# Two attention and MLP layers on one core: reordered first and last stages in place of a pre-scaled third term of VectorE's exponential

## The chip, the cores and the metric

The kernel runs on one core of one Trainium2 chip. The metric is the device time of one execution in microseconds. Before the change the median of three runs is 1617.62 us (1613.32 to 1618.33); the profiled execution, on which all positions in this text are based, took 1613.32 us and has a span of 1611.5 us from the first to the last instruction. TensorE had a mean granted clock of 0.997.

## The reference

Two rounds of the same two blocks, with the same weights, on x of 2048 rows and 512 columns in bf16. There are 32 heads of 16 columns, and the MLP has 1792 hidden columns.

```python
def _A_ref(x, wqkv, wo):                     # attention
    qkv = (x @ wqkv).reshape(B, S, 3, H, Dh).transpose(2, 0, 3, 1, 4)
    q, k, v = qkv[0], qkv[1], qkv[2]
    scores = jnp.einsum("bhqd,bhkd->bhqk", q, k) * (Dh ** -0.5)
    p = _softmax(scores, axis=-1)
    o = jnp.einsum("bhqk,bhkd->bhqd", p, v)
    return o.transpose(0, 2, 1, 3).reshape(B, S, D) @ wo

def _B_ref(x, w1, w2):                       # MLP
    h = jnp.maximum(x @ w1, 0)
    return h @ w2

x = A_x
x = x + _A_ref(_layernorm(x), A_wqkv, A_wo)
x = x + _B_ref(_layernorm(x), B_w1, B_w2)
x = x + _A_ref(_layernorm(x), A_wqkv, A_wo)
x = x + _B_ref(_layernorm(x), B_w1, B_w2)
```

The heads are narrow and the rows many: per layer there are 32 x 2048 x 2048 exponentials, and they are the largest single piece of work.

## The kernel before

Scores are computed with the keys on the partitions: 128 keys by 512 queries of one head are one block, which fills one bank of PSUM (128 x 512 fp32). A *slot* is up to three blocks in one of two PSUM tiles `ps_s` of three banks. ScalarE (ACT in the profile) takes the exp of a slot into one of five buffers `e`, and TensorE multiplies that with the values into `ps_o` (32 partitions per head, four heads side by side); a column of ones beside the values gives the sum for the division. The kernel's Python code holds its own model of the engines' clocks and uses it to decide, slot by slot, in what order to emit score products, value products and all the projection and MLP work that fills TensorE in between.

Some slots hand their third block to VectorE (DVE), which works out the exponential itself. Two such blocks of 512 columns make a *pair* of 128x1024. The score, scaled to powers of two, is turned into a 16-bit integer whose bits, read as bf16, are a straight-line 2^x (`lin`); the same bits with the mantissa masked off are the power of two below it (`step`); and a cubic of the mantissa is the third part (`cube`). The exponential is the sum of the three, and since the value product is linear, TensorE adds them up: three value products for a block of VectorE's against one for a block of ScalarE's. The factor `CUBE` of the third part can be put on the part itself or on the values:

```python
    CUBE, SUM = 0.1667, 2.16619
    THIRD = (8, 9, 10, 11)
    vthird = {kb: sb([P, H // 2, PW], BF16, f"vthird_{kb}") for kb in THIRD}
    # scale_v: vthird[kb] = vaug[l][kb] * CUBE, one operation of 128x544 per kb and layer
    ...
    def pv(sg, kb, g, rhs, p=None):
        values = vthird[kb] if p and p["scaled"] else vaug[sg["l"]][kb]
        nc.tensor.matmul(ps_o[32 * g : 32 * g + 32, 0 : sg["w"]],
            values[:, 4 * sg["T"] + g, 2 * e : 2 * e + 32], rhs, ...)
    ...
    def chain(p):      # after both halves of lin are there
        steps = (
            (342, lambda: bits(0x7F, 0x3F80)),                           # mantissa into step
            (609, lambda: nc.vector.tensor_mul(out=power, in0=mantissa, in1=mantissa)),
            (342, lambda: nc.vector.tensor_scalar(
                out=power, in0=power, scalar1=CUBE, scalar2=None, op0=ALU.mult)),
            (342, lambda: bits(0x7F80, 0)),                              # step
            (609, lambda: nc.vector.tensor_mul(
                out=power.bitcast(BF16), in0=power, in1=line.bitcast(BF16))),
        )
        nos = (0, 1, 3, 4) if p["scaled"] else range(5)
```

For a pair whose two blocks both lie in key blocks 8 to 11, the third product uses the scaled values and the chain leaves out the scaling. The choice of the block for VectorE prefers such key blocks, and looks ahead in the list of units for one. A pair begins only if the model finds VectorE's queue (`BACKLOG`, `queued`) short enough for it to be done in time.

The layer norm takes its inverse root on VectorE from an integer first guess and, at the two ends of the kernel, three Newton steps there:

```python
    def ln_stats(tag, tt, i):
        nc.vector.bn_stats(out=st[:], in_=x_t[tt][:])
        nc.vector.bn_aggr(out=mv[ln_n(tag)][:, i, :], in_=st[:])
    def ln_rstd(tag, part):     # part 0: 3 operations; parts 1 to 3: a Newton step of 3 each
```

The first stage, up to the first exp:

```python
    idle_matmuls(18)            # keep TensorE's clock up; another one behind each transpose
    for i in range(TPC): ln_stats(tag, i, i)
    for part in range(4): ln_rstd(tag, part)
    for i in range(TPC): ln_apply(tag, i, i)
    for i in range(TPC):        # transpose, copied by VectorE (even i) and ScalarE (odd i)
        ...
    b = plain(k_mms(0, 0));     nc.scalar.copy(out=ktp[0][0][0][:], in_=b)
    b = plain(q_mms(0, 0, 0));  q_masked(0, b, 0); q_masked(0, b, 1)       # VectorE
    for kb in range(2):
        b = plain(v_mms(kb));   nc.scalar.copy(out=v_out(0, kb), in_=v_in(b))
```

The last stage, after the loop over the slots, works on the last 256 rows (two tiles of 128, `rows`):

```python
    while seg_at[0] < len(segs):
        force_v(); run_dve(0.0, musts)        # last value products, copy of ps_o to u
    ending[0] = True
    run_all()                                 # all groups still waiting
    for i in rows:                            # residual + products with wo of 7 of 8 parts
        add(banks[i], ident[:], x_t[tt + i][:], True, False)
        for t in range(NT - 1):
            add(banks[i], ot[t][:, part(i)], wo[:, t // 2, :], False, False)
    for i in rows:
        last_steps[0](i)                      # shuffle of u (once), reciprocal, product -> ot[7]
        add(banks[i], ot[NT - 1][:, part(i)], wo[:, (NT - 1) // 2, :], False, True)
        nc.scalar.copy(out=x_t[tt + i][:], in_=at_bank(banks[i]))
    for i in rows: ln_stats(tag, tt + i, i)
    for step in range(4): ln_rstd(tag, step)
    for i in rows: ln_apply(tag, tt + i, i)
    half_part(0, range(NF))                   # output of an earlier tile of rows
    ...                                       # transposes; then the last MLP, 14 steps:
    for ft in range(NF + 1):
        ... w1buf[n % NW1][:, c, :] ...       # 4 buffers; load_w1(n + NW1) refills behind each
    ...                                       # two copies, two stores from SyncE's queue
```

The softmax here doesn't subtract the row's maximum and nothing guards it: scores larger than these inputs give would overflow.

## Time and profile before

| | ScalarE | VectorE | TensorE | GpSimd |
|---|---|---|---|---|
| busy, us of 1611.5 | 1566.0 | 1496.8 | 1451.6 | 93.8 |
| instructions | 1387 | 3007 | 14667 | 279 |

| stage, us from the start of the span | what happens | length |
|---|---|---|
| 0 to 16.81 | loads, first layer norm, first keys, queries and values | 16.81 |
| 16.81 to 1577.83 | 1366 exps on ScalarE, everything else beside them | 1561.02 |
| 1577.83 to 1611.50 | last normalisation, last layer norm, last MLP, stores | 33.67 |

The stages are cut at the start of the first exp and at the end of the last. The profile names an operation by its line, its engine, what it writes and reads (`e<-ps_s`: from a PSUM tile of scores into a buffer of exponentials), its shape and its count; then follow the busy time, the mean duration of one in ns, and the idle time of the engine just before, with what ended it. Neighbouring operations on one engine overlap, so a mean duration can be longer than the step from one start to the next, and 703 x 1573 ns is more than the 1052.1 us in which any of those exps was running. A timeline row has the start and the length in us, the engine and line, the operation, and a count if neighbours are merged; in brackets stands the idle time before it and what released it. In the rows of the stages, each engine has its busy time and, in brackets, its number of instructions; the last three numbers are TensorE's granted clock, the share of the DMA engines and the GB/s moved.

### The profile page before, as it was taken

How to read it: one execution, taken by the hardware profiler on the slowest of the kernel's cores; microseconds unless marked ns; L12 is line 12 of the kernel's file. 1: busy time of each engine (PE TensorE's matmuls, PEld its weight loads, DVE VectorE, ACT ScalarE, POOL GpSimd, SP SyncE). 2: the span in 40 equal slices, each digit the busy share in tenths (PEclk: the TensorE clock that was granted, in tenths of full speed). 3: DMA queues.
4: the chain of work that ended last, by engine and by line, in shares of the span. 5: the costliest groups of instructions: out<-in, count | busy, mean ns of one | idle time of the engine just before them, and what ended most of it. 6: DMA issues, size and time to landing. Idle time of an engine off the chain costs nothing.

```text
span 1611.5 us, 35252 instructions
## 1 busy us (share of the span) xinstructions
PE 1451.6 (90%) x14667; PEld 508.9 (32%) x14863; DVE 1496.8 (93%) x3007; ACT 1566.0 (97%) x1387; POOL 93.8 (6%) x279
## 2 busy tenths in 40 slices
PE   8888888999989999899998998888989999899997
PEld 3222222322222222222222222222333333344444
DVE  7669999999999999999898998999999999999994
ACT  6999999999999999999999999999999999999993
POOL 2000001001010011000100000001001010010100
PEclk9999999999999999999999999999999999999999
DMA  5000000210002100021000100000210111121223
GB/s 164 1 1 2 2 2 10 46 28 12 5 18 45 21 15 9 12 47 25 9 1 17 31 1 1 2 3 9 44 30 16 26 29 36 22 48 36 47 46 73
DMA packets 113889, 39.97 MB, mean 25 GB/s; under 512 B 103328, under 2 KB 111264, under 8 KB 113728
## 3 DMA queue, kind: packets, MB, share of 16 engines
q1 hardware_dynamic: 101696, 26.21, 7.1%
q0 software_dynamic: 10688, 10.18, 3.4%
q8 instruction: 116, 1.90, 0.5%
q10 hardware_dynamic: 1344, 1.31, 0.2%
q14 instruction: 45, 0.37, 0.1%
HBM read 24.38 MB, written 2.10 MB: 16 GB/s over the span
## 4 chain that ended last, share of the span: by engine, by line
ACT 78%; PE 11%; DVE 7%; issue 3%; DMA 1%; ACTq 0%; DVEq 0%
ACT e L1311 78%; PE ps_s L1302 4%; PE ps_o L901 3%; PE ps_f L434 3%; DVE lin L995 2%; DVE step L1036 1%; PE ps_s L1365 1%; DVE cube L1047 1%; DVE cube L1051 1%; DVE stats L465 0%; DVE ht L682 0%; DVE q L625 0%; DVE ot L836 0%; DVE x L708 0%; DMA c<-u 0%
## 5 line engine op out<-in xcount | busy, mean ns | idle before, releaser
L1311 ACT ACTIVATE e<-ps_s 128x1024 bf16<-128x1024 f32 (+1 forms) x1366 | 1554.8, 1367 | 6.6 <-PE ps_s L1302 4.7
L1302 PE MATMUL ps_s<-q,ktp 32*128 32x512 bf16 (+1 forms) x6060 | 601.2, 341 | 106.7 <-ACT e L1311 84.7
L901 PE MATMUL ps_o<-e,vaug 128*32 128x512 bf16 (+1 forms) x4284 | 494.7, 345 | 11.3 <-DVE u L823 4.8
L995 DVE TENSOR_SCALAR lin<-ps_s 128x512 int16<-128x512 f32 x662 | 452.6, 686 | 35.8 <-PE ps_s L1302 30.4
L1302 PEld LDWEIGHTS <-ktp 32*128 32x128 bf16 x6060 | 189.9, 91 | 504.5 <-issue 375.6
L1036 DVE TENSOR_SCALAR step<-lin 128x1024 int16<-128x1024 int16 x662 | 262.9, 420 | 3.3 <-PE ps_o L901 0.6
L901 PEld LDWEIGHTS <-vaug 128*32 128x32 bf16 x6004 | 161.5, 94 | 302.2 <-issue 291.5
L1047 DVE TENSOR_TENSOR cube<-step 128x1024 f16<-128x1024 bf16 x331 | 225.9, 685 | 2.7
L1051 DVE TENSOR_TENSOR cube<-cube,lin 128x1024 bf16<-128x1024 f16 x331 | 225.5, 682 | 0.0
L901 PE MATMUL ps_o<-step,vaug 128*32 128x512 bf16 (+1 forms) x836 | 143.2, 340 | 0.3 <-issue 0.3
L901 PE MATMUL ps_o<-cube,vthird 128*32 128x512 bf16 (+1 forms) x788 | 138.2, 337 | 0.6 <-issue 0.3
L901 PE MATMUL ps_o<-lin,vaug 128*32 128x512 bf16 (+1 forms) x836 | 127.4, 338 | 4.1 <-DVE u L823 2.8
L434 PE MATMUL ps_f<-xnT,w 128*128 128x512 bf16 (+1 forms) x446 | 116.9, 345 | 5.6 <-issue 2.5
L434 PE MATMUL ps_f<-w,ht 128*128 128x512 bf16 x334 | 104.8, 384 | 5.6 <-issue 4.3
L850 POOL DMA_DIRECT2D r<-u x52 | 37.5, 721 | 1165.9 <-DVE step L1036 424.3
L434 PE MATMUL ps_f<-xnT,wqkv 128*128 128x512 bf16 (+1 forms) x288 | 82.3, 359 | 6.4 <-issue 2.5
L682 DVE TENSOR_SCALAR ht<-ps_f 128x512 bf16<-128x512 f32 x103 | 70.7, 687 | 3.2 <-PE ps_f L434 3.0
L434 PE MATMUL ps_f<-wo,ot 128*128 128x512 bf16 x206 | 65.4, 384 | 3.0 <-issue 1.9
L625 DVE TENSOR_SCALAR q<-ps_f,qmask 128x512 bf16<-128x512 f32 (+1 forms) x102 | 64.8, 661 | 3.1 <-PE ps_f L434 3.0
L434 PEld LDWEIGHTS <-w 128*128 128x128 bf16 x504 | 39.1, 97 | 60.0 <-issue 50.6
L836 DVE SCALAR_TENSOR_TENSOR ot<-u,mask,r 128x512 bf16<-128x512 f32 (+2 forms) x82 | 51.3, 627 | 1.1
L901 PEld LDWEIGHTS <-vthird 128*32 128x32 bf16 x788 | 39.8, 95 | 32.8 <-issue 30.1
(91 smaller groups left out, 609.8 us busy)
## 6 DMA issues: line engine op xcount, KB each, us to landing
w<-in_B_w_dram SPq DMA_DIRECT2D x140, 128.0 KB
r<-u POOLq DMA_DIRECT2D x25, 256.0 KB, 7.1
r<-u POOLq DMA_DIRECT2D x27, 128.0 KB, 4.5
out_dram<-x SPq DMA_DIRECT2D x16, 128.0 KB
x<-in_A_x_dram SPq DMA_DIRECT2D x14, 128.0 KB
w<-in_B_w_dram SPq DMA_DIRECT2D x1, 1792.0 KB
wqkv<-in_A_wqkv_dram ACTq DMA_DIRECT2D x2, 512.0 KB
c<-u SPq DMA_DIRECT2D x48, 8.0 KB
```

Of the source, the lines that this page charges most:

```text
L434: nc.tensor.matmul(out, lhsT, rhs, start=i % k == 0, stop=i % k == k - 1)
L625: return nc.vector.tensor_scalar(out=qbuf[n % 2][e][:, 0:w], in0=b, scalar1=qmask[e][:, 0:1], scalar2=None, op0=ALU.mult,)
L682: nc.vector.tensor_scalar(out=out, in0=sums, scalar1=0.0, scalar2=None, op0=ALU.max)
L836: nc.vector.scalar_tensor_tensor(out=ot[t][:, at_column + a : at_column + a + w], in0=u[:, a : a + w], scalar=mask[e][:, 0:1], in1=r[:, a ...
L850: nc.gpsimd.dma_start(out=r[:, 0:width], in_=bass.AP(tensor=sums.tensor, offset=sums.offset, ap=[list(sums.ap[0]), [0, 32], [1, width]],),)
L901: nc.tensor.matmul(ps_o[32 * g : 32 * g + 32, 0 : sg["w"]], values[:, 4 * sg["T"] + g, 2 * e : 2 * e + 32], rhs, start=g not in sg["begun" ...
L995: first = nc.vector.tensor_scalar(out=lin[which][:, half * QS : (half + 1) * QS], in0=src, scalar1=EXP_BIAS, scalar2=0.0, op0=ALU.add, op1 ...
L1036: nc.vector.tensor_scalar(out=stair, in0=line, scalar1=keep, scalar2=put, op0=ALU.bitwise_and, op1=ALU.bitwise_or,)
L1047: (609, lambda: nc.vector.tensor_mul(out=power, in0=mantissa, in1=mantissa)),
L1051: (609, lambda: nc.vector.tensor_mul(out=power.bitcast(BF16), in0=power, in1=line.bitcast(BF16))),
L1302: nc.tensor.matmul(b[:, a : a + sg["w"]], kt[32 * g : 32 * g + 32, kc : kc + P], qbuf[sg["n"] % 2][sg["e"]][32 * g : 32 * g + 32, 0 : sg[" ...
L1311: ex = nc.scalar.activation(out=eb[:, 0 : place[m]], in_=b[:, 0 : place[m]], func=ACTF.Exp, scale=1.0 / (LOG2E * UNIT),)
```

## The change

Two things of different kinds are exchanged.

*Taken out* is the pre-scaled third part: `THIRD`, the scaled value copies, their eight scaling operations, the search for blocks in those key blocks, and the chain of four operations; every pair has all five again.

*Put in* is a set of measures at the two ends, to shorten the chains there. At the start the statistics of four tiles run one behind the other and are aggregated together; the inverse root takes a cubic first step and one Newton step (nine operations with the first guess, in place of twelve); the idle products between the transposes go; the first value block is copied by VectorE between the two query masks, and the second comes later. At the end the residual products of one row of tiles stand ahead of the last value product, the last normalisation reads PSUM instead of a copy, and groups that still wait are emitted behind the layer norm. The MLP's first weights are kept for the last stage: four in their buffers and ten in buffers of the first layer's keys, which are free by then. MLP inputs have a buffer of their own, `xn2T`. The last store but one and the last are issued from two engines.

Cut to its core (`...` marks cuts):

```diff
+GAIN = 64.0 / 9.0
-    THIRD = (8, 9, 10, 11)
-    vthird = {kb: sb([P, H // 2, PW], BF16, f"vthird_{kb}") for kb in THIRD}
+    xn2T = sb([P, NDC, QS], BF16, "xn2T")
...
-        nc.vector.bn_stats(out=st[:], in_=x_t[tt][:])
-        nc.vector.bn_aggr(out=mv[ln_n(tag)][:, i, :], in_=st[:])
+        nc.vector.bn_stats(out=stats[ln_n(tag)][:, i, :], in_=x_t[tt][:])
+    def ln_seed(tag, rows, gain=1.0):        # aggregates of all rows, then 2 operations
+    def ln_root(tag, rows):                  # seed, then 7 operations on VectorE
+        nc.vector.tensor_mul(out=t1, in0=y, in1=y)
+        nc.vector.tensor_mul(out=t1, in0=t1, in1=a)
+        stt(out=t1, in0=t1, scalar=-10.0 / 3.0, in1=t1, op0=ALU.add, op1=ALU.mult)
+        stt(out=y, in0=t1, scalar=5.0, in1=y, op0=ALU.add, op1=ALU.mult)
+        stt(out=t1, in0=y, scalar=-0.5 / GAIN, in1=y, op0=ALU.mult, op1=ALU.mult)
+        nc.vector.tensor_mul(out=t1, in0=t1, in1=a)
+        stt(out=y, in0=t1, scalar=1.5, in1=y, op0=ALU.add, op1=ALU.mult)
...
-        if n < len(chunks) * NF:
+        if n < len(chunks) * NF - NF + NW1:                       # load_w1
...
+        if (l, j) == (1, LAST - 2):                               # weights of the last stage
+            for ft in range(NF): ... w1_last.append(home); if ft >= NW1: nc.sync.dma_start(out=home, ...)
...
-        nos = (0, 1, 3, 4) if p["scaled"] else range(5)
+        for n, (cost, fn) in enumerate(steps):
...
-    idle_matmuls(18)
+    idle_matmuls(21)
-        copy = nc.scalar.copy if i % 2 else nc.vector.tensor_copy
+        copy = nc.vector.tensor_copy if i > 1 else nc.scalar.copy
-        idle_matmuls(1)
...
+    uses(q_masked(0, q_bank, 0), at_q)
+    b = plain(v_mms(0))
+    uses(nc.vector.tensor_copy(out=v_out(0, 0), in_=v_in(b)), in_bank[0])
+    uses(q_masked(0, q_bank, 1), at_q)
-    for kb in range(2):
-        b = plain(v_mms(kb))
-        uses(nc.scalar.copy(out=v_out(0, kb), in_=v_in(b)), in_bank[0])
...
-        order = sorted(sg["kbs"], key=lambda kb: len(sg["kbs"]) == NKB and kb in THIRD)
-        for kbs in zip(*[iter(order)] * both):
+        for kbs in zip(*[iter(sg["kbs"])] * both):
...
-        for sg, kb, g in now:
-            run_until(("v", sg["l"], kb))                         # values ready before each slot
...
+    first_part(0)                                                 # residual products, row 0
+    while seg_at[0] < len(segs):
+        force_v()                                                 # last value product
+        run_dve(0.0, musts)
+    first_part(1)
     for i in rows:
         last_steps[0](i)                                          # now reads ps_o, not u
...
+    ln_root(tag, n_rows)
     for i in rows:
         ln_apply(tag, tt + i, i)
+    ending[0], wide[0] = True, False
+    run_all()                                                     # stood ahead of all this before
...
-        nc.sync.dma_start(
+        (nc.scalar if i % 2 else nc.sync).dma_start(
```

## The prediction

> **What bounds the kernel now.** I read the page's busy line first, then the chain that ended last, then the span cut into three stages at the first and last exp, then the groups by shape, and last the timeline of the two ends.
>
> ```profile
> PE 1451.6 (90%) x14667; PEld 508.9 (32%) x14863; DVE 1496.8 (93%) x3007; ACT 1566.0 (97%) x1387; POOL 93.8 (6%) x279
> ...
> ACT 78%; PE 11%; DVE 7%; issue 3%; DMA 1%; ACTq 0%; DVEq 0%
> ```
>
> ScalarE (ACT) is busy for 97% of the span and makes 78% of the chain; VectorE (DVE) comes next with 93%. The stage view (length, then busy time and count of each engine) separates three parts:
>
> ```profile
> 0.00:16.81 16.81, 12.57 (x60) 5.50 (x61) 13.16 (x42) 4.42 (x7) 2.41 (x35) 1.00 0.78 252
> 16.81:1577.83 1561.02, 1412.80 (x14450) 488.82 (x14642) 1471.17 (x2931) 1554.85 (x1366) 91.40 (x244) 1.00 0.10 21
> 1577.83:1611.50 33.67, 26.25 (x166) 14.61 (x160) 12.43 (x35) 6.72 (x14) 0.00 (x0) 0.97 0.29 71
> ```
>
> Between the first exp at 16.81 us and the end of the last at 1577.83 us ScalarE runs 1366 exps and nothing else, with 1561.02 - 1554.85 = 6.2 us idle. That stage is as long as its exps are wide. The other two stages, 16.8 and 33.7 us, are chains of dependent work in which ScalarE hardly counts. So I add up three separate changes: the width of the exps, the start, the end. The groups by shape carry the first:
>
> ```profile
> L1311 ACT ACTIVATE e<-ps_s 128x1536 bf16<-128x1536 f32 x703 | 1052.1, 1573 | 4.5 <-PE ps_s L1302 2.8 <-PE ps_o L901 1.2
> L1311 ACT ACTIVATE e<-ps_s 128x1024 bf16<-128x1024 f32 x662 | 717.7, 1148 | 2.1 <-PE ps_s L1302 1.9 <-PE ps_o L901 0.2
> L995 DVE TENSOR_SCALAR lin<-ps_s 128x512 int16<-128x512 f32 x662 | 452.6, 686 | 35.8 <-PE ps_s L1302 30.4
> L1036 DVE TENSOR_SCALAR step<-lin 128x1024 int16<-128x1024 int16 x662 | 262.9, 420 | 3.3 <-PE ps_o L901 0.6
> L1047 DVE TENSOR_TENSOR cube<-step 128x1024 f16<-128x1024 bf16 x331 | 225.9, 685 | 2.7
> L1051 DVE TENSOR_TENSOR cube<-cube,lin 128x1024 bf16<-128x1024 f16 x331 | 225.5, 682 | 0.0
> L1048 DVE TENSOR_SCALAR cube<-cube 128x1024 f16<-128x1024 f16 x24 | 10.1, 420 | 0.2
> ```
>
> Each slot has three score blocks of 512 columns. In 703 slots ScalarE takes all three; in 662 it takes two and VectorE one. VectorE joins two such blocks to a pair, so there are 331 pairs, and only 24 of them need the scaling step of line 1048.
>
> **What the Trainium skill says.** "Perfetto Trace Analysis", section Identifying the Most-Contended Engine, says to improve the engine with the highest occupancy; the trace agrees that it is ScalarE, with VectorE so near that it matters who does which block. The same page, Optimizing Scalar/DVE Operations, says that both engines pay a fixed cost per instruction, so larger operations are cheaper per element. The trace agrees: 512 more columns add 1573 - 1148 = 425 ns to an exp, though two thirds of the wider exp's duration would be 1049 and not 1148. "VectorE: DVE Perf Modes", The perf-mode tier table, gives a one-source operation in SBUF a faster mode than one with two tensors; the trace has 420 ns for the scaling against 682 to 685 for the products. "DMA: Bandwidth & Descriptors", Issuing engines are not separate DMA queues, says that a second issuing engine saves the issue alone; no run here has shown it.
>
> **Part 1: the third part of VectorE's pairs goes.** Without the scaled copy of the values every pair needs the scaling again. The scheduler that writes the program, seeing a longer queue, gives VectorE fewer pairs. The instruction list of the changed program has 749 exps of 1536 columns, 616 of 1024 and one of 512, 308 pairs and 308 scalings.
>
> ScalarE: 46 exps become 512 columns wider. By the mean durations that is 46 x 0.425 = 19.6 us. The step between exps gives a check: the first 18, all wide, take 24.28 us, so (24.28 - 1.57) / 17 = 1.336 us a step; the 662 narrow ones then have (1560.2 - 703 x 1.336) / 662 = 0.938, and 46 x 0.398 = 18.3 us. I take **+19 us**, all on the bound.
>
> VectorE, by the same mean durations: gone are 46 x 0.686 + 46 x 0.420 + 23 x 1.367 = 82 us and 2.3 us of scaled copies; new are 284 x 0.420 = 119 us. That is +35 us of durations; they overlap, with operations of 128x512 starting 0.60 us apart where one lasts 0.69, so about +25 to +30 us of occupied time. In an exp stage of 1580 us VectorE goes from 1471 / 1561 = 94% to about 95%. TensorE has 92 fewer value products of a block, four of which run side by side: about 5 us less. Neither ends the stage, so I count nothing for them.
>
> **Part 2: the start.** The lines of the head that set the first exp:
>
> ```profile
> 6.72 0.18 DVE L466 BATCH_NORM_AGGREGATE mv<-stats 128x2 f32<-128x6 f32 x1
> ...
> 9.32 1.38 DVE L507 TENSOR_SCALAR xn<-x,mv,ya 128x512 bf16<-128x512 bf16 x4
> ...
> 14.10 1.41 DVE L625 TENSOR_SCALAR q<-ps_s,qmask 128x512 bf16<-128x512 f32 x2 [0.17 <-PE ps_s L1103]
> ...
> 16.37 0.39 PE L1302 MATMUL ps_s<-q,ktp 32*128 32x512 bf16 x3
> ```
>
> Four statistics in a row, then four aggregates, save three waits of about 0.1 us, and nine small operations replace twelve at 0.2 us: apply starts near 8.5, not 9.32. The transposes follow it without idle matmuls between, and ScalarE's two copies come first: I put the key product at 10.8 us, where it was 12.18. Key and query take 1.9 us (12.7). VectorE then does the first mask (to 13.4), the copy of the first values (to 14.4) and the second mask (to 15.0). The score product waits for that second mask, since its bank is in the tile that the scores overwrite. Before, the mask ended at 15.5, but TensorE worked off eleven value products first and scores began at 16.37. So scores at 15.1, exp 0.44 later: 15.5, **-1.3 us**.
>
> **Part 3: the end.** E is the end of the last exp.
>
> ```profile
> 1583.98 0.38 PE L1365 MATMUL ps_s<-x,ident 128*128 128x512 bf16 x1 [0.85 <-DVE x L708]
> ...
> 1587.85 1.07 ACT L1375 CAST x<-ps_s 128x512 bf16<-128x512 f32 x2 [7.10 <-PE ps_s L1365]
> ...
> 1592.59 0.74 DVE L507 TENSOR_SCALAR xn<-x,mv,ya 128x512 bf16<-128x512 bf16 x2
> ...
> 1594.39 1.03 PE L1365 MATMUL ps_s<-xnT,w 128*128 128x256 bf16 x8 [0.39 <-DVE xnT L1406]
> ```
>
> Before: two MLP groups and one output group hold TensorE until the residual products can start at E+6.2; the copies come at E+10.0, apply at E+14.8, the last MLP at E+16.6. After: the first row's eight products (1.7 us) run beside the last exp, the last value product follows near E+1.2 and ends at E+1.7. The shuffle reads PSUM directly. Shuffle, two reciprocals and two products took 1583.85 to 1586.91, 3.06 us: done at E+4.8. Last product and copy of the second row: E+5.8. Its statistics 0.7, aggregate and nine small operations 2.1: apply at E+8.7. TensorE meanwhile has the rest of one output group and all of the other, 9 + 15 products of 0.22 us, until about E+10.4, later than apply; so transposes start there, and after 1.2 us of copies the last MLP starts at E+11.6: -4.9 us. Its weights are all in place, so the wait for them at 1601.70 goes (0.31 us on TensorE, about 0.5 in step): -0.5. The two last stores issue from two engines, where one took 0.83 us for both: -0.2. Together **-5.6 us**.
>
> **Sum.** +19 - 1.3 - 5.6 = +12 us on the median 1617.62: about 1629.5; I say 1629.
>
> **The rivals.** *The stage was losing time to waits, which go.* Pairs go wherever the scheduler can fit blocks, and the old rule, every value product's input ready before the slot, is dropped. For it: in the trace the shortest steps between exps are 1.330 and 0.904 us, so 1561 us holds about 27 us over 703 x 1.330 + 662 x 0.904. Against it: ScalarE's idle time is 6.2 us, and nothing in the change aims at the rest. If half of the 27 went, 1616. *VectorE becomes the bound.* For it: a fifth step in nearly every pair, 95% busy, and 84.7 us in which scores wait for exps show how tightly the buffers turn. Late lines hold score banks, and ScalarE then idles. Against it: the program has 23 fewer pairs just for that. It would cost 10 to 20 us more: 1640 to 1650. *The start is held by a transfer.* The first values are now ahead of the second mask, and their weights are the last part of that load to arrive, at 12.7 us in the trace before, just when I need them. It would cost up to 1 us.
>
> **Range and chances.** The exp term is a count times a measured step, good to about 1 us if the waits stay; the waits may move by 8 either way; the ends are good to 2; the runs before span 1613.3 to 1618.3. That gives 1620 to 1640. Faster by 2% means under 1585, which no rival reaches; slower by 2% means over 1650, which only a late VectorE reaches.
>
> **What would show it.** Exp stage about 1580 us with 749 wide exps and under 10 us idle; first exp near 15.5; last exp to the end near 28 us, the last MLP starting some 11.6 us after the last exp with no wait for weights. I am wrong if the step of a wide or narrow exp moves by over 10 ns, or if scores wait for VectorE's lines.

## The result and the profile after

The changed kernel takes 1629.52 us (median of 4 runs, 1628.83 to 1631.42); the kernel before, run beside it, 1615.47 (4 runs). The ratio is 1.0089, with a 95% interval of 1.0065 to 1.0113: slower by about 14 us, and within 2%. The prediction was 1629.0.

The busy line and the chain by engine, from the page of the changed kernel:

```profile
PE 1457.4 (90%) x14553; PEld 509.3 (31%) x14743; DVE 1507.5 (93%) x3126; ACT 1583.3 (97%) x1383; POOL 93.9 (6%) x279
...
ACT 77%; DVE 10%; PE 9%; issue 2%; DMA 1%; POOL 0%; SPq 0%; ACTq 0%; DVEq 0%
```

ScalarE still bounds the kernel, and it is busy 17.3 us longer (1566.0 before). The three stages, cut again at the first exp and at the end of the last (length, then busy time and count of each engine, TensorE's clock, DMA share, GB/s):

```profile
0.00:16.83 16.83, 12.26 (x52) 5.06 (x54) 11.07 (x34) 3.15 (x5) 2.42 (x35) 0.90 0.84 266
16.83:1599.45 1582.62, 1421.92 (x14361) 491.70 (x14548) 1485.11 (x3062) 1574.67 (x1366) 91.50 (x244) 1.00 0.10 22
1599.45:1627.90 28.45, 23.26 (x141) 12.55 (x142) 11.36 (x31) 5.52 (x13) 0.00 (x0) 1.00 0.06 19
```

The exp stage is 21.6 us longer, the last stage 5.2 us shorter, and the first, in this execution, the same. The groups by shape:

```profile
L1298 ACT ACTIVATE e<-ps_s 128x1536 bf16<-128x1536 f32 x749 | 1116.9, 1594 | 10.5 <-PE ps_s L1289 8.3 <-PE ps_o L914 2.0
L1298 ACT ACTIVATE e<-ps_s 128x1024 bf16<-128x1024 f32 x616 | 678.2, 1169 | 1.5 <-PE ps_s L1289 1.3
L1021 DVE TENSOR_SCALAR lin<-ps_s 128x512 int16<-128x512 f32 x616 | 421.4, 687 | 25.5 <-PE ps_s L1289 20.0 <-issue 0.2
...
L1069 DVE TENSOR_TENSOR cube<-step 128x1024 f16<-128x1024 bf16 x308 | 210.7, 686 | 1.5 <-PE ps_o L914 0.3
L1073 DVE TENSOR_TENSOR cube<-cube,lin 128x1024 bf16<-128x1024 f16 x308 | 210.1, 683 | 0.0
L1070 DVE TENSOR_SCALAR cube<-cube 128x1024 f16<-128x1024 f16 x308 | 129.2, 421 | 1.0
```

749 wide exps instead of 703, 308 pairs instead of 331, and the scaling in every pair at 421 ns. The shortest steps from one exp to the next are those of before, 1.330 us for 1536 columns and 0.904 for 1024. With them 46 wider exps are 46 x 0.426 = 19.6 us. What the stage takes above the sum of its shortest steps I call its **waits**: 26.8 us before, 28.8 now. 19.6 + 2.0 is the 21.6.

The head, from the timeline of the changed kernel:

```profile
8.07 1.38 DVE L504 TENSOR_SCALAR xn<-x,mv,ya 128x512 bf16<-128x512 bf16 x4
...
10.52 3.31 PE L1121 MATMUL ps_s<-xnT,wqkv 128*128 128x512 bf16 x8 [0.62 <-DMA x<-in_A_x_dram]
...
15.60 0.74 DVE L612 TENSOR_SCALAR q<-ps_s,qmask 128x512 bf16<-128x512 f32 x1
...
16.39 0.40 PE L1289 MATMUL ps_s<-q,ktp 32*128 32x512 bf16 x3 [1.44 <-DVE q L612]
```

Apply starts 1.25 us earlier (9.32 before) and the key product at 10.52, both 0.3 to 0.4 us earlier than predicted. Then eight products take 3.31 us, where 1.89 was expected. Three cuts through the head show why; the last three columns are TensorE's granted clock, DMA share and GB/s:

```profile
10.00:12.00 2.00, 1.48 (x5) 0.61 (x6) 1.56 (x4) 0.04 (x1) 0.00 (x0) 0.70 0.76 225
12.00:14.00 2.00, 2.00 (x6) 0.68 (x5) 0.13 (x1) 0.59 (x1) 0.00 (x0) 0.50 0.73 219
14.00:16.00 2.00, 0.95 (x4) 0.34 (x3) 1.63 (x3) 0.00 (x0) 0.00 (x0) 0.94 0.92 285
```

The clock was down to half; in the kernel before it was 1.00 in all three cuts. So the gain of the start was lost in this execution. Other programs with the same head, below, kept it; of the changed kernel itself no other execution was profiled.

The tail, E being the end of the last exp at 1599.45:

```profile
1601.59 0.44 DVE L879 STREAM_SHUFFLE r<-ps_o 128x256 f32<-128x256 f32 x1
...
1605.13 0.59 ACT L1366 CAST x<-ps_s 128x512 bf16<-128x512 f32 x1 [0.66 <-PE ps_s L1349]
...
1607.09 3.19 PE L1349 MATMUL ps_s<-w,ht 128*128 128x512 bf16 x14
...
1608.48 0.73 DVE L504 TENSOR_SCALAR xn<-x,mv,ya 128x512 bf16<-128x512 bf16 x2
...
1610.12 0.61 PE L513 MATMUL ps_s<-ident,xn 128*128 128x128 bf16 x8
...
1611.44 1.03 PE L1349 MATMUL ps_s<-xn2T,w 128*128 128x256 bf16 x8 [0.28 <-ACT xn2T L1399]
```

The shuffle starts at E+2.1 (E+6.0 before), the second copy at E+5.7, apply at E+9.0, and the last MLP at E+12.0 instead of E+16.6. Apply ended 0.9 us before the transposes began: TensorE was busy with an output group (the 14 products), as predicted.

### The profile page after: what moved, and what is told of

It is laid out like the page before. It is cut to its first block, busy times and chain, and to the rows that moved or that the text cites. A ratio compares the mean times of both kernels' runs of the same rounds, so it can differ in the third digit from the quotient of the medians.

```text
span 1627.9 us, 35135 instructions
## 1 busy us (share of the span) xinstructions
PE 1457.4 (90%) x14553; PEld 509.3 (31%) x14743; DVE 1507.5 (93%) x3126; ACT 1583.3 (97%) x1383; POOL 93.9 (6%) x279
## 4 chain that ended last, share of the span: by engine, by line
ACT 77%; DVE 10%; PE 9%; issue 2%; DMA 1%; POOL 0%; SPq 0%; ACTq 0%; DVEq 0%
ACT e L1298 77%; DVE lin L1021 3%; PE ps_s L1289 3%; PE ps_o L914 2%; PE ps_f L430 2%; DVE step L1061 1%; DVE cube L1069 1%; PE ps_s L1349 1%; DVE cube L1073 1%; DVE cube L1070 1%; DVE q L612 0%; DVE ht L669 0%; DMA u<-c 0%; DMA wqkv<-in_A_wqkv_dram 0%; DVE ot L843 0%
## 5 line engine op out<-in xcount | busy, mean ns | idle before, releaser
L1298 ACT ACTIVATE e<-ps_s 128x1536 bf16<-128x1536 f32 (+1 forms) x1366 | 1574.7, 1402 | 12.0 <-PE ps_s L1289 9.6
L914 PE MATMUL ps_o<-e,vaug 128*32 128x512 bf16 (+1 forms) x4340 | 516.9, 346 | 13.6 <-DVE u L827 4.6
L1021 DVE TENSOR_SCALAR lin<-ps_s 128x512 int16<-128x512 f32 x616 | 421.4, 687 | 25.5 <-PE ps_s L1289 20.0
L1061 DVE TENSOR_SCALAR step<-lin 128x1024 int16<-128x1024 int16 x616 | 246.1, 421 | 0.9 <-PE ps_o L914 0.7
L1069 DVE TENSOR_TENSOR cube<-step 128x1024 f16<-128x1024 bf16 x308 | 210.7, 686 | 1.5 <-PE ps_o L914 0.3
L1073 DVE TENSOR_TENSOR cube<-cube,lin 128x1024 bf16<-128x1024 f16 x308 | 210.1, 683 | 0.0
L914 PE MATMUL ps_o<-cube,vaug 128*32 128x512 bf16 (+1 forms) x780 | 145.5, 341 | 0.5 <-issue 0.5
L1070 DVE TENSOR_SCALAR cube<-cube 128x1024 f16<-128x1024 f16 x308 | 129.2, 421 | 1.0
L430 PE MATMUL ps_f<-xn2T,w 128*128 128x512 bf16 (+1 forms) x457 | 121.1, 343 | 9.5 <-DVE ht L669 3.6
L612 DVE TENSOR_SCALAR q<-ps_f,qmask 128x512 bf16<-128x512 f32 (+1 forms) x102 | 65.1, 662 | 10.1 <-PE ps_f L430 7.9
L843 DVE SCALAR_TENSOR_TENSOR ot<-u,mask,r 128x512 bf16<-128x512 f32 (+1 forms) x78 | 49.8, 640 | 0.9
```

The source lines that it names most:

```text
L430: nc.tensor.matmul(out, lhsT, rhs, start=i % k == 0, stop=i % k == k - 1)
L612: return nc.vector.tensor_scalar(out=qbuf[n % 2][e][:, 0:w], in0=b, scalar1=qmask[e][:, 0:1], scalar2=None, op0=ALU.mult,)
L843: nc.vector.scalar_tensor_tensor(out=ot[t][:, at_column + a : at_column + a + w], in0=u[:, a : a + w], scalar=mask[e][:, 0:1], in1=r[:, a ...
L914: nc.tensor.matmul(ps_o[32 * g : 32 * g + 32, 0 : sg["w"]], vaug[sg["l"]][kb][:, 4 * sg["T"] + g, 2 * e : 2 * e + 32], rhs, start=g not in ...
L1021: first = nc.vector.tensor_scalar(out=lin[which][:, half * QS : (half + 1) * QS], in0=src, scalar1=EXP_BIAS, scalar2=0.0, op0=ALU.add, op1 ...
L1061: nc.vector.tensor_scalar(out=stair, in0=line, scalar1=keep, scalar2=put, op0=ALU.bitwise_and, op1=ALU.bitwise_or,)
```

## The experiments

Each compares with the kernel before, run on the same chip. Some have short names below: third_out and third_in are the kernels with the third part taken out and put back, new_start and new_end those with one end of the change alone, and combined is the changed kernel with the third part and the early pairs. Where I write of waits, first exp or last stage, they are from the profile of that kernel, counted as above.

### The third part alone taken out

```diff
 (the kernel before)
-    THIRD = (8, 9, 10, 11)
+    THIRD = ()
```

> The kernel before with the pre-scaled third part taken out and nothing else changed: no key block counts as scaled, so every pair does its own scaling. The program has 739 exps of 1536 columns and 626 of 1024 (703 and 662 before), 313 pairs. If the width of the exps is all that counts: 36 x 0.41 = +15 us in the exp stage, so about 1576 us of it, first and last stage as before (16.8 and 33.7 us), some 15 us or 0.9% slower than before. If VectorE became the bound, ScalarE's idle time in the stage rises above 15 us and the time is 25 us or more above before. If the stage had waits to win back, it is under 8 us slower. The changed kernel has 10 blocks fewer on VectorE than this one, so part of its exp time would then come from something else than the third part.

Measured: 1629.32 us, ratio 1.0091 (1.0075 to 1.0107), which is the whole loss. But the program has 739 wide exps, not 749:

```profile
L1311 ACT ACTIVATE e<-ps_s 128x1536 bf16<-128x1536 f32 x739 | 1106.5, 1586 | 5.0 <-PE ps_s L1302 3.0 <-PE ps_o L901 1.7
```

Its exp stage:

```profile
16.70:1596.15 1579.45, 1451.08 (x14561) 492.62 (x14561) 1503.21 (x3106) 1569.75 (x1366) 91.25 (x244) 1.00 0.10 21
```

So the third part accounts for 36 of the 46. 36 x 0.426 = 15.3 us, waits 29.9 (+3.1), last stage 30.4 instead of 33.7 (-3.2): together the 15.1 us by which the profiled span grew. What the change puts in is then worth nothing on the whole, though its last stage is 2 us shorter than this one's. Something in it must cost what its ends gain.

### The third part put back into the changed kernel

```diff
 (the changed kernel; the last norm's own buffer xn2T makes room for it)
+    THIRD = (8, 9, 10, 11)       # and scaled copies, four-step chains, search for blocks, as before
-    xn2T = sb([P, NDC, QS], BF16, "xn2T")
```

> The changed kernel with the pre-scaled third part put back; so that it fits in SBUF, the MLP inputs go back into the attention's buffers instead of one of their own. 715 exps of 1536 columns and 650 of 1024, 325 pairs. If the width of the exps counts: 34 x 0.42 = 14 us less than the changed kernel, exp stage about 1568 us, first exp still near 16.8, last stage about 28.4 us; about 1615 us, within 3 us of the kernel before (5 us more exp, 5 us less end). If the new measures at the ends and the third part got in each other's way, more than 1622.

Measured: 1642.85 us, ratio 1.0182 (1.0159 to 1.0205). A clear miss. With 715 wide exps the widths cost only 5 us over before; the waits are 45.2 us, 15.1 of them between 800 and 900 us, about where the layers change. And the last stage is 40.7 us: the scheduler had put off seven hidden-layer groups of eight products behind the last exp, and three of them waited for weights on top. From its timeline (the bracket gives the idle time before the row, and what ended it):

```profile
1608.64 1.11 PE L435 MATMUL ps_s<-xnT,w 128*128 128x256 bf16 x8 [1.10 <-DMA w<-in_B_w_dram]
...
1613.02 1.05 PE L435 MATMUL ps_f<-xnT,w 128*128 128x256 bf16 x8 [1.55 <-DMA w<-in_B_w_dram]
```

The parts of the change don't add up in any order, because each of them makes the scheduler write another program for all of the 1580 us. From here on I count waits and what is left for the end in every run.

### The scaling left out

```diff
 (the changed kernel; the same order of everything else, but no scaling in any pair, so the output is another)
-            (342, lambda: nc.vector.tensor_scalar(
-                out=power, in0=power, scalar1=CUBE, scalar2=None, op0=ALU.mult)),
+            (342, lambda: None),
```

> The changed kernel's program in the same order, but the scaling of the cubic part is left out of every pair (the output differs; 308 VectorE operations of 0.42 us are not there). Exps stay at 749, 616 and 1. If VectorE is not the bound: exp stage within 4 us of the changed kernel's 1582.6. If VectorE's lateness costs time: the stage shrinks by 10 to 28 us towards 749 x 1.330 + 616 x 0.904 = 1553. The head is that of the changed kernel: if TensorE's low clock there is a fixed feature of that order, it shows again between 10.4 and 14 us.

Measured: 1628.33 us, ratio 1.0088 (1.0067 to 1.011). Its exp stage:

```profile
15.22:1598.75 1583.53, 1456.40 (x14548) 492.28 (x14547) 1400.72 (x2754) 1574.17 (x1366) 91.23 (x244) 1.00 0.11 23
```

VectorE has 84 us less to do and the stage is as long as ever (1583.5 against 1582.6). With its 308 pairs, in its order, the changed kernel isn't bound by VectorE. The head has the changed kernel's order, the clock stayed at 1.00, and the first exp came at 15.22: the low clock is not a feature of that order.

### A warm head

```diff
 (the changed kernel)
         mark(("xnT", tag, i))
+        idle_matmuls(1)          # an idle product behind each transpose, as in the kernel before
```

> The changed kernel with one idle product behind each of the four transposes of the first stage put back, as the kernel before had. If the missing products let TensorE's clock drop (0.50 to 0.63 between 10.4 and 14 us in the changed kernel, key and query products 3.3 us instead of 1.9): clock 1.0 there, key and query in 1.9 us, first exp near 15.5 us instead of 16.83, whole time 1.3 us less. If the clock is not what held the start, but a transfer or VectorE's order: first exp still at 16.8.

Measured: 1629.43 us, ratio 1.0095 (1.0072 to 1.0119), first exp at 15.71. The clock stayed up in this execution, but so it did in seven programs with the new start and without these products; what they do for the clock is not shown. All eight other programs with the new start have their first exp between 15.19 and 15.77, those with the old start between 16.70 and 16.88. So, against the 16.81 of before, the start saves 1.0 to 1.6 us, unless the clock falls. The rival that a transfer holds the start was small where it was seen: in combined the first value product waited 0.45 us for its weights.

### The pairs of before, with the scaling in every one

```diff
 (the kernel before; its order and its 331 pairs; the scaled copies are made but not used)
-        values = vthird[kb] if p and p["scaled"] else vaug[sg["l"]][kb]
+        values = vaug[sg["l"]][kb]
...
+            if p["scaled"] and n == 1:
+                fn = lambda: (steps[1][1](), steps[2][1]())
```

> The kernel before with its order and its 331 pairs, but the scaling instruction (0.42 us) is run in every pair, and the value copies that made it unnecessary are not used. Rival (VectorE becomes the bound): 307 more scalings are 129 us more of VectorE in a stage where it already works 90 per cent; if VectorE could not hold 331 pairs without the third part, the time rises well above 1629, towards 1640 to 1700. Theory (the pairing rule gives up pairs, not the engine): a scaling is 0.42 us, 307 x 0.42 = 129 us, VectorE's 1485 us of busy time in the changed kernel plus 23 pairs x 3.7 us = 85 us would be about 1570 of 1580 us, which is too full for a schedule without waits: I expect 1625 to 1640 us, that is no gain from keeping the pairs. A time of 1616 would say that the pairs were given up needlessly.

Measured: 1716.0 us, ratio 1.0625 (1.0604 to 1.0647), far above what I expected. Its exp stage, and the group of all its exps:

```profile
16.78:1679.05 1662.27, 1447.31 (x14450) 485.05 (x14642) 1580.82 (x3238) 1588.53 (x1366) 95.26 (x244) 0.98 0.09 20
```

```profile
L1313 ACT ACTIVATE e<-ps_s 128x1024 bf16<-128x1024 f32 (+1 forms) x1366 | 1588.5, 1270 | 74.1 <-PE ps_s L1304 64.0
```

VectorE has 109.6 us more of busy time, and the stage is 101.2 us longer. ScalarE idles 74.1 us before its exps (6.6 before), 64.0 of them for scores, and the chain that ended last runs through VectorE:

```profile
DVE 74%; ACT 13%; PE 10%; issue 3%; DMA 1%; DVEq 0%
```

So in this order VectorE is the bound. The order was made for chains of four operations, and how much of the 101 us is due to that is not shown: VectorE's share of the stage is 95.1% here and 95.2% in third_out, which has an order made for five operations and only 3.1 us more waits than before. But VectorE's 1580.82 us of busy time alone is as long as the changed kernel's exp stage (1582.62). As an estimate from this, no order of 331 pairs with five operations would have been much faster than the changed kernel; the scheduler doesn't give up the pairs needlessly.

### The early start of the pairs put back

The changed kernel lets a pair begin only when the last value block is there. The kernel before let the first begin as soon as some keys were.

```diff
 (the changed kernel)
-... ((mine['l'] or ("v", 0, 15) in made) and ...
+... ((mine['l'] or ("v", 0, 15) in made or not pairs and ("k", 0, 0, 1) in made) and ...
```

> The changed kernel with one condition of before put back: pairs may start as soon as the first layer's keys of the first columns are there, instead of when the last value block is there. Theory: of the 46 exps that became 512 columns wider, 36 come from the missing third part (the kernel with the third part alone taken out has 739 wide and 626 narrow exps) and 10 from this condition. Putting it back should give again about 739 wide and 626 narrow exps, which is 10 x (1.330 - 0.904) = 4.3 us less of exps; time 1625 us, ratio to before 1.006. Rival: the early pairs only delay the first value groups and the first exps wait for them, so the time stays at 1629.

Measured: 1639.56 us, ratio 1.0154 (1.0139 to 1.0169). 743 wide exps, six fewer, but waits of 41.9 us instead of 28.8. In this program the rule is a gain of some 10 us, and my theory had its sign wrong. Of the 13.1 us more waits, 7.4 lie between 100 and 200 us; the run of the new start alone, below, shows what these are.

### The old order at the end

```diff
 (the changed kernel; waiting groups and residual products after the last value product, as before)
-    first_part(0)
     while seg_at[0] < len(segs):
         force_v()
         run_dve(0.0, musts)
+    ending[0], wide[0] = True, False
+    run_all()
+    ending[0], wide[0] = False, True
+    first_part(0)
     first_part(1)
...
-    ending[0], wide[0] = True, False
-    run_all()
-    ending[0], wide[0] = False, True
```

> The changed kernel with the residual products and the waiting groups placed after the last value product, as before. Theory: the last stage (28.5 us from the end of the last exp) gets back what the order gave, the shuffle and the row copies come no earlier, and the last MLP starts about 3 to 5 us later: last stage 31 to 33 us. Rival: the gain of the last stage came from the kept MLP weights and the root alone; then it stays at 28.5 us.

Measured: one run, 1629.68 us; last exp at 1599.51, last stage 28.4 us.

```profile
1602.64 0.44 DVE L879 STREAM_SHUFFLE r<-ps_o 128x256 f32<-128x256 f32 x1
...
1609.63 0.74 DVE L504 TENSOR_SCALAR xn<-x,mv,ya 128x512 bf16<-128x512 bf16 x2
...
1610.11 0.72 PE L513 MATMUL ps_s<-ident,xn 128*128 128x128 bf16 x8 [0.72 <-DVE xn L504]
...
1611.43 1.03 PE L1349 MATMUL ps_s<-xn2T,w 128*128 128x256 bf16 x8 [0.18 <-DVE xn2T L1399]
```

Shuffle and apply come 1.0 and 1.1 us later than in the changed kernel, as they should, and the last MLP starts at E+11.9 all the same. With the old order the transposes wait for VectorE's norm and start at E+10.6; with the new one they follow TensorE's last group and start at E+10.7. With so little work left over, the two chains are equally long, and the order gains nothing. Neither my 31 to 33 us nor the attribution in the prediction holds.

### The old root at the end

```diff
 (the changed kernel)
-    ln_root(tag, n_rows)
+    ln_seed(tag, n_rows)
+    for _ in range(3): ...       # three Newton steps, nine operations instead of seven
```

> The changed kernel with the three Newton steps of before for the root in the last stage, 9 dependent instructions instead of 7. Theory: the transposes start when TensorE's groups are done (10.7 us after the last exp), not when apply is (9.0 us), so a root that is about 0.2 to 0.5 us longer changes nothing: last stage 28.5 us within 0.3. Rival: the root lies on the chain; then the last stage is longer by the 0.2 to 0.5 us that apply comes later.

Measured: one run, 1630.02 us; E is 1599.79, apply at 1609.21, which is E+9.4 instead of E+9.0, and the last MLP at 1611.77, E+12.0. Last stage 28.45 us. The 0.4 us disappear in the same slack.

### The new end alone

```diff
 (the kernel before; third part, pairs and start untouched)
+    # the shuffle reads ps_o; residual products ahead of the last value product;
+    # waiting groups behind the last norm; ln_root instead of three Newton steps
```

> The kernel before, third part and pairs and start as they were, with only the end of the changed kernel: the last shuffle reads the sums in PSUM without a copy, the residual products stand ahead of the last value product, the waiting output groups come after the last norm, and the other root. MLP weights are loaded again as before. Theory: the order of the exps is untouched, so the last exp ends at 1577.8 as in before; in the last stage the shuffle comes 2.1 to 3 us after the last exp instead of 6.0, apply follows 7 us later, and TensorE still has the one or two hidden-layer groups that before left for the end, 2.8 us more than the changed kernel: the last MLP starts 13 to 14.5 us after the last exp instead of 16.6. Last stage 30 to 32 us instead of 33.7, time 1612 to 1614, ratio 0.998. Rival: the 5 us of the last stage came from the fewer groups and the kept weights alone; then the last stage stays within 0.5 us of 33.7 and the ratio is 1.000.

Measured: 1613.79 us, ratio 0.9994 (0.9983 to 1.0005). The last exp ends at 1577.66, so E+2.1 for the shuffle and E+8.9 for apply are what the changed kernel has. But:

```profile
1583.05 1.04 PE L435 MATMUL ps_f<-xnT,w 128*128 128x256 bf16 x8
...
1583.92 1.04 PE L435 MATMUL ps_s<-xnT,w 128*128 128x256 bf16 x8
...
1586.59 0.73 DVE L534 TENSOR_SCALAR xn<-x,mv,ya 128x512 bf16<-128x512 bf16 x2
...
1591.90 0.61 PE L543 MATMUL ps_s<-ident,xn 128*128 128x128 bf16 x8
...
1593.23 1.03 PE L1401 MATMUL ps_s<-xnT,w 128*128 128x256 bf16 x8 [0.28 <-ACT xnT L1451]
```

Apply is done at 1587.3 and the transposes start at 1591.90, after the two hidden-layer groups that this schedule leaves for the end and the output groups behind them. The last MLP starts at E+15.6: 1.0 us gained. That is less than a tenth of a percent, and within the interval of the ratio.

### All but the changed kernel's pair rule, with the third part

```diff
 (the changed kernel)
+    THIRD = (8, 9, 10, 11)       # as in the run third_in, without xn2T
+... or not pairs and ("k", 0, 0, 1) in made ...       # early pairs, as before
-... rest + (0.0 if first["j"] == NQS - 1 and not first["l"] ...
+... rest + (-8.0 if first["j"] == NQS - 1 and not first["l"] ...
```

> The changed kernel with the third part put back, with the early start of the pairs and the -8 in the pace of before put back too, and without the buffer of its own for the last norm's transposes. It has 711 wide and 654 narrow exps (before 703 and 662), and few groups are left behind the last exp, as in the changed kernel. Theory: exps as in before plus 8 x (1.330 - 0.904) = 3.4 us, start 1.0 to 1.6 us earlier, last stage 28.5 us instead of 33.7: 1615.5 + 3.4 - 1.3 - 5.2 = 1612.4, if the exps wait no more than the 27 us of before. Rival: the start with later value blocks makes the exps wait, as in the kernel with the third part put back, which lost 16 us in waits, and in the one with early pairs, which lost 11: then 1622 to 1628.

The pace says how much waiting work of the projections and the MLP the scheduler adds behind each slot; the changed kernel lacks the -8 that the kernel before had for the last columns of the first layer. Measured: 1625.98 us, ratio 1.0073 (1.006 to 1.0086). First exp 15.54, last stage 28.3, 711 wide exps, all as foreseen; but the waits are 42.5 us, 10.1 of them between 100 and 200 us (1.9 before). The rival was right.

### The new start alone

```diff
 (the kernel before; third part, early pairs, pace and end untouched)
+    # first norm, keys and queries, one value block ahead of the first exp, as in the changed kernel
-        for sg, kb, g in now:
-            run_until(("v", sg["l"], kb))
```

> The kernel before with only the start of the changed kernel (first norm with the other root, keys and queries ahead of all but one value block, no wait for value blocks ahead of an exp), third part, early pairs, pace and end as before. It has the 711 wide and 654 narrow exps of the kernel called combined, and fewer output groups left behind the last exp than before. Theory: the start is gained (first exp 15.5 instead of 16.8) and paid back with interest: 8 x (1.330 - 0.904) = 3.4 us of wider exps and some 10 us of waits around 110 us, where the value groups that were put off meet the early pairs. Last exp at 1596, last stage 30 to 31 us as in the kernel without the third part, which has the same end; time 1628, ratio 1.0085. Rival: the loss of the combined kernel lies in its end or in the kept weights' loads; then the last exp of this one comes at about 1580 and its time is 1612 to 1616.

The edit takes along the changed norm in the whole kernel, so the last stage has the new root too. Measured: 1625.77 us, ratio 1.0064 (1.0045 to 1.0082). The first exp comes at 15.19 us, 1.6 earlier than before, and the last exp at 1594.46, 16.6 later. Waits 41.6 us, 14.8 more than before, of which 7.2 lie between 100 and 200 us and 3.9 behind one wait at 1210 us (5.3 us, where before has one of 1.4); wider exps 8 x 0.426 = 3.4. The largest of the first lot, in the timeline:

```profile
105.01 0.38 PE L518 MATMUL ps_f<-ident,xn 128*128 128x128 bf16 x4 [0.52 <-DVE xnT L560]
...
105.91 1.87 PE L435 MATMUL ps_f<-xnT,wqkv 128*128 128x512 bf16 x4 [0.51 <-DVE xnT L560]
...
107.81 0.69 DVE L577 CAST ktp<-ps_f 128x512 bf16<-128x512 f32 x1 [1.96 <-PE ps_f L435]
...
108.56 0.60 PE L1316 MATMUL ps_s<-q,ktp 32*128 32x512 bf16 x2 [0.25 <-DVE ktp L577]
...
109.27 1.02 ACT L1325 ACTIVATE e<-ps_s 128x1024 bf16<-128x1024 f32 x1 [4.18 <-PE ps_s L1316]
```

The last block of first-layer keys isn't there when the scores need it. Its cast comes at 107.81 us here, and within 0.6 us of that in the two other kernels with new start and early pairs; it comes at 97.98 in the kernel before and at 96.21 in the changed kernel, which holds the pairs back. Its four transposes and VectorE's copies take turns on one bank, 0.9 us a turn, then follow the key product, the cast, the scores. In the kernel before, the same transposes ran between 91.3 and 95.3 us, with exps going on beside them. And TensorE, waiting for about half of the time in that chain, loses half its clock. Cuts of 3 us (third column from the end is the clock; ScalarE's busy time is the fourth of the five):

```profile
101.00:104.00 3.00, 1.79 (x20) 0.93 (x18) 2.33 (x5) 3.00 (x4) 0.00 (x0) 1.00 0.00 0
104.00:107.00 3.00, 1.86 (x11) 0.93 (x11) 0.91 (x3) 1.08 (x1) 0.00 (x0) 0.73 0.00 0
107.00:110.00 3.00, 2.75 (x13) 0.34 (x11) 1.45 (x3) 0.73 (x1) 0.00 (x0) 0.50 0.00 0
110.00:113.00 3.00, 3.00 (x20) 0.75 (x16) 1.59 (x3) 1.88 (x3) 0.00 (x0) 0.63 0.00 0
```

In the kernel before the clock is 1.00 in all of these cuts. The runs with early pairs and with all combined show the same stall at the same place (4.18 and 4.38 us before one exp) and the same clock. The four products of the key took 1.87 us there, against 1.04 us at full clock in an earlier block of the same run. The wait at 1210 us is another thing: there the exps wait for value products, and these for a cubic part from VectorE; why the new start brings it is open.

This kernel's last stage is 29.5 us with before's order at the end: it has no hidden-layer group left behind the last exp, and its last MLP starts at E+11.9.

### The new end with kept weights

```diff
 (the kernel called new_end)
+        if (l, j) == (1, LAST - 2): ... w1_last.append(home) ...    # last MLP's weights stay in SBUF
-            load_w1(n + NW1)
-        nc.sync.dma_start(
+        (nc.scalar if i % 2 else nc.sync).dma_start(                # last two stores
```

> The kernel before with the end of the changed kernel, as in the run called new_end (1613.79, ratio 0.9994), and the last MLP's weights kept in SBUF instead of loaded again, and the second store issued by ScalarE. Theory: between the start of the last MLP and the end, before has 17.1 us, new_end 17.3 and the changed kernel 16.5; the kept weights and the store are worth this 0.6 to 0.9 us, nothing else moves: last stage 32.1 instead of 32.9, ratio 0.9985 to 0.999. Rival: the earlier loads of these weights collide with nothing and are hidden, but so were the late ones: 32.9 and no gain.

Measured: 1614.3 us, ratio 0.9992 (0.9979 to 1.0005). The last stage is 32.0 us instead of 32.9, as foreseen. But in its profiled execution the last exp ended at 1581.45, 3.8 us later than in new_end, with the same exps in the same order. Two stretches of both, new_end first, then this one:

```profile
230.00:240.00 10.00, 8.37 (x79) 2.29 (x76) 9.76 (x20) 10.00 (x10) 0.00 (x0) 1.00 0.02 2
590.00:612.00 22.00, 19.72 (x180) 6.65 (x173) 20.84 (x46) 21.23 (x20) 3.67 (x12) 0.92 0.05 11
```

```profile
230.00:240.00 10.00, 8.38 (x65) 1.89 (x64) 8.69 (x18) 9.12 (x9) 0.00 (x0) 0.83 0.01 1
590.00:612.00 22.00, 20.43 (x163) 5.85 (x163) 18.38 (x39) 19.45 (x18) 3.65 (x12) 0.77 0.07 13
```

The clock fell where it had not, or less, in the other run, and ScalarE was busy 2.7 us less in these two stretches. Such dips come and go between executions and hide a gain of 0.9 us. They also tell how far to trust the waits of one profile: 26.7 us in new_end and 30.4 here, so a difference of 2 or 3 us, as between before and the changed kernel, shows nothing. Neither this kernel nor new_end can be told from the kernel before; no version tried is measurably faster than it.

## Why the prediction was right, and where not

The four kernels with third part and start varied form a square, in parts of the time before:

| | old start | new start |
|---|---|---|
| with the third part | 1 | 1.0064 |
| without it | 1.0091 | 1.0154 (early pairs; with the new end and another pace too) |

1.0091 + 1.0064 - 1 = 1.0155: within the intervals, some 3 us each, the two costs add, +14.7 and +10.3 us on 1615. The sum is rough, since the last corner differs in the end as well. The later pairs then take 1.0154 down to the changed kernel's 1.0089, -10.5 us. That makes the +14 measured, but -10.5 is no property of the rule. With the third part in, the kernel with late pairs (third_in, 1.0182) is slower than the one with early pairs (combined, 1.0073); the two differ in the pace as well, and which of the two does it is not separated.

- **The exp term, +19.** Count and step held: 749 wide exps, 0.426 us each, 21.6 us of stage with waits. Its cause was only partly right. The third part's absence makes 36 of the 46 wider exps. The other ten come from the rest of the change: six from the rule for the pairs (743 and 749), about four from the rest, mainly the new start (739 and 743; with the third part in, the new start alone makes eight). I had laid all of them on the third part.
- **VectorE not the bound.** Right for 308 pairs, shown by leaving the scaling out. The reason given for it, that the program has 23 fewer pairs for that purpose, is borne out in the main: the third part alone costs 18 of them, and the kernel that kept 331 in an order made for shorter chains took 1716 us. The prediction's price for this rival was 10 to 20 us; there it is 100. The sum for VectorE was off: I had 25 to 30 us more of occupied time and 95% of the stage, where the profile has 13.9 us more (1471.17 to 1485.11) and 93.8%.
- **The start, -1.3.** Right in size, 1.0 to 1.6 us in the eight other programs with this start; in the changed kernel's profile TensorE's clock fell to half and the gain was lost. The step that failed is taking the start by itself. In the program that the scheduler makes of it, the first layer's last keys come too late for early pairs. The three kernels with both have 13 to 16 us more waits than the changed kernel or the one before; some 7 to 8 of them lie between 100 and 200 us, where these keys are late, and the rest is not traced in full. The changed kernel holds the pairs back and avoids them. The prediction doesn't name that rule at all, while it decides between 1629 and 1640.
- **The end, -5.6.** 5.2 us in the profile, with every time of the chain within 0.5 us of its step. The path held: TensorE's groups end last, at E+10.7 where I had E+10.4. What failed is the credit to the edited lines. The order of residual products and groups is worth nothing here (E+11.9 with the old order), nor is the root. Everything put in at the end is worth 1.1 to 1.7 us: last stage 29.5 against 28.3 us in new_start and combined, 33.7 against 32.0 in the kernel before and the new end with kept weights. Of this, 0.9 to 1.1 us comes after the start of the last MLP, from the kept weights and the stores, where I had 0.7. The other 3.5 to 4.1 us are TensorE's leftover work: it is busy 13.5 us between the last exp and the last MLP before, 10.7 us now. Two hidden-layer groups and part of an output group, with the wait behind them, are what the new schedule happens to finish before the last exp. The old order with another schedule gives E+11.9 as well, in new_start. The kernel without the third part, also with the old end, leaves no hidden-layer group but the whole output group, and starts at E+13.8.
- **The rival of waits that go** fell: 28.8 us against 26.8. The range's allowance of 8 us for waits was wide enough for the kernel as it is, and too narrow for its neighbours (41.6 to 45.2 in four of them).

So the total was right partly by luck. The counts came from the list of the changed program, but that the waits would stay was an assumption, and it held only because two unnamed things, the start's waits and the pair rule, cancel. The half microsecond between 1629.0 and 1629.52 is luck as well: I added +12 to a median of 1617.62, and the measured +14 stands on 1615.47. What stays open is why two of the seven schedules leave hidden-layer groups behind the last exp (two groups in before, seven in third_in); nothing in them asks for it, and I could only count it.

Where the prediction rests on the shape of an exp's cost, the Trainium skill has it too: "ScalarE: Activation LUTs", What ACT_TABLE_LOAD costs, gives 0.833 ns per element of a partition's row. The trace agrees: (1.330 - 0.904) us over 512 columns is 0.832 ns.

## What to carry to other kernels

When a program comes out of a scheduler, a change at one end is a change everywhere: count for each version the instructions on the bound, the waits above their shortest steps, and the work left behind for the end, before giving a gain to the lines that were edited. A chain at the end is only shortened on the engine that finishes last, here TensorE with its leftover groups and not VectorE's norm. And moving work out of the way of a start only defers it: look for the first place where its result is due.

## What the runs showed of the hardware

TensorE's granted clock can fall without a long wait. In the cuts of the new start alone it was 1.00 and then 0.73 in two stretches of 3 us in which TensorE was busy 1.79 and 1.86 us; transposes and copies took turns there, and no single wait was longer than about half a microsecond. In the next two it was 0.50 and 0.63, although TensorE was busy for 2.75 and 3.00 us of them. It did so at the same place in three programs, and in the changed kernel's head in its profiled execution and not in the eight other programs with this start. "TensorE: Matmul & The Clock Gate", section What's actually happening, knows a half-rate state set by recent activity in a free-running window, which fits the 0.50 and the chance in it; no run here isolates what decides. A stall that leaves TensorE half idle is therefore paid twice: the key product that ended this chain took 1.87 us instead of 1.04.

An engine's share of busy time did not tell whether it was the bound. VectorE was busy for 95.2% of the exp stage in third_out, whose waits are 29.9 us, and for 95.1% in the kernel with 331 pairs of five operations, where scores came late and ScalarE idled 74.1 us.
